# Idle products among the first scores, later empty rows, the last pair's first scores set between older value products, and four late transposes in one go, in an attention and mixture-of-experts kernel

## The chip, the cores and the metric

The kernel runs as one program on one core of a Trainium2 chip. The metric is the device time of that program in microseconds (us). Before the change three timed runs gave 710.47, 710.98 and 714.45 us, median 710.98 us. One further execution was profiled: it took 711.56 us, and the profile of it covers a span of 709.5 us from the first to the last instruction.

## The reference, cut to what matters

Attention over q, k, v of 4 batches, 8 heads, 768 tokens and 64 numbers per head. Each token gets six hash bits per head (the signs of a product with `proj`), and a query only sees keys of the same bucket. Every one of the 3072 tokens then goes to one of eight experts:

```python
mask = q_bucket[:, :, :, None] == k_bucket[:, :, None, :]
scores = np.where(mask, scale * np.matmul(q, k.transpose(0, 1, 3, 2)), -1e9)
attn = softmax(scores)                       # max, exp, sum, divide
x = np.matmul(attn, v)                       # tokens x 512 over all heads
expert_idx = np.argmax(x @ w_gate, axis=1)   # one expert per token
y[rows of e] = relu(x[rows of e] @ w1[e]) @ w2[e]
out = gate_w[:, None] * y
```

## The kernel before

**Pairs, units, halves.** The 32 heads are worked off in 16 pairs (`g` from 0 to 15, `NG` = 16). A pair has twelve units; a unit is 128 queries of one head against all 768 keys. Two heads' units make halves `u` = 2g and 2g+1 of the queries. For a unit, TensorE computes the scores into a PSUM tile "s" (`score`, lines 309 and 311: a sum of two products, since q and k are split into a high and a low part; the hash masks sit in sixteen extra rows of the split tile). VectorE takes the maximum (`peak`, L319) and two small factors (L324, L326; on some units GpSimd does them, L324 and L328), ScalarE takes the exponential (`expo`, L335). Half of the units are turned by TensorE transposes (`trans`, L349) and copied out (`trans_ev`, L375 on ScalarE or L373 on VectorE), the others by VectorE (`turn`, L389) and 16 DMAs from SBUF to SBUF (`exchange`, L400). The value products (`pv`, L411) collect six steps per half in a PSUM tile "t"; ScalarE copies the result (`pv_end`, L416), and `tok` (L430) brings it into token order. There are three "s" tiles and two "t" tiles.

**Masks.** The hash bits of a pair are computed one pair ahead (`lsh_mm`, L264), written to DRAM by SyncE (L278) and read back into the split tiles by two DMAs that GpSimd issues (`mask`, L282), behind its splitting work for the next pair (lines 192 to 233). The first score of a pair needs the mask of the pair's first head, and that is the later of the two reads. Pair 0 makes its bits in place (`lsh_first`, L239, `bits_first`, L250 on VectorE and L244 on ScalarE).

**What sets the order.** Each engine runs its own queue in order, and that order is written out by hand: a table of words per pair, read by `step`. `HEAD` is for pair 0, `PLAN` for pairs 1 to 14, `LAST` for pair 15. A word is a letter and a number: S score, R maximum, A factor, X exponential, T transpose, E its copy, B three steps of a value product, O its end, K and L the token product and its scaling, D and Y the VectorE turn and the exchange, Z and N routing; in `HEAD` also y (L239), b (bits), k j q l p (splitting) and f (the first score in two parts); in `LAST` also m, u, d (first expert: product, relu, its low part), n and t (a weight's high and low part, L941 and L949) and r, c (routing and scatter). A minus sign means the pair before, two mean the one before that. So "B11-" in the table of pair 14 is the second half of the value product of half 1 of pair 13.

**Empty rows.** Each expert has a region of rows in DRAM (`xs`, tile name "sorted_rows"). `fill(e)` (L150) writes 512 empty rows of expert e, one DMA of 1156 KB, issued on SyncE; `before`, called at every even score, says at which.

**First expert's rows.** Once all tokens are scattered, the rows of an expert are loaded (`rows`), transposed and split into a high and a low part (`xt`: L750 on TensorE, L755 on ScalarE, L756 on VectorE for the first expert's two groups of 256 rows; tile "xhe"), multiplied by w1 (`mm1`, L769) and by w2 (`mm2`, `yout`, L867), scaled (L878) and scattered to the output. Phases 0 and 1 are the two groups of the first expert. For phase 1 the kernel before transposes the first two of four blocks in the middle of the last w2 product of phase 0, and the other two behind it, all into "t" tiles:

```python
mm2(0, 1, lambda: xts(1, (0, 1)))
xts(1, (2, 3))
```

`warmth` (L106) issues products of a tile of ones with itself, 512 columns in bf16; ten of them run at the start.

Of the kernel before, what the change touches and what calls it, by code (L numbers as in the profile page):

```python
# [7 lines left out]
F32 = mybir.dt.float32  # L8
# [7 lines left out]
B, H, S, D = 4, 8, 768, 64  # L16
# [3 lines left out]
NG = B * NP  # L20
# [11 lines left out]
M0 = float(2 ** 34)  # L32
# [18 lines left out]
def tiles_of(n):  # L51

    return [(o, min(128, n - o)) for o in range(0, n, 128)]
# [3 lines left out]
def lsh_attention_moe(ctx, tc, qk2, v, proj, wg, w1, w1q, w2, out):  # L57
# [3 lines left out]
    ps = ctx.enter_context(tc.tile_pool(name="ps", bufs=1, space=bass.MemoryType.PSUM))  # L61
# [658 lines left out]
    def tokens(n):  # L720
        r, o, c = PH[n]
        IX[n] = moe.tile([128, 4], I32, name="ix", bufs=3)
        t = len(tiles_of(c))
        x = XI[n][:, :t, 1] if n > 1 else XG[n][:, :t, GC + 1]
        nc.vector.tensor_copy(IX[n][:, :t], x.bitcast(I32))

    def heads(x, d):

        return x[:, d * PW + E:d * PW + E + 2 * D]
# [9 lines left out]
    def xt(n, d):  # L739
        r, o, c = PH[n]  # L740
        if d == 0:
            XH[n] = (moe.tile([128, 2, 4, EARLY], F32R, name="xhe") if n < 2 else
                     P2["p"].tile([128, 2, 4, CAPS[1]], F32R, name="xh"))
        t = len(tiles_of(c))
        if n > 1:
            p = XT[n][:, d]
        else:
            p = ps.tile([128, 512], F32, name="t", bufs=2)
            for j in range(t):
                nc.tensor.transpose(p[:, j * 128:(j + 1) * 128], heads(XG[n][:, j], d), ident)  # L750
        if d == 0:
            GT[n] = moe.tile([128, 4], F32, name="gate", bufs=3)
            nc.vector.tensor_copy(GT[n][:, :t], XI[n][:, :t, 0] if n > 1 else XG[n][:, :t, GC])
            tokens(n)
        nc.scalar.activation(XH[n][:, 0, d, :c], p[:, :c], AF.Copy)  # L755
        nc.vector.tensor_tensor(XH[n][:, 1, d, :c], p[:, :c], XH[n][:, 0, d, :c], op=OP.subtract)  # L756

    LEN = {}

    def length(n):  # L760

        r = PH[n][0]
        LEN[n] = nc.values_load(C["ni"][0:1, r:r + 1], engines=[mybir.EngineType.PE], min_val=0, max_val=N)

    def products(n, p, c, terms):

        def part(z, ts, first):
            for k, (w, x) in enumerate(ts):
                nc.tensor.matmul(p[:, :z], w, x[:, :z], start=first and k == 0, stop=k == len(ts) - 1 and (n < 2 or not first))  # L769
# [5 lines left out]
        part(c, terms[:1], True)  # L775
        with tc.If(LEN[n] > z[2]) as more:
            with tc.If(LEN[n] > z[1]) as most:
                part(z[0], terms[1:], False)
            with most.Else():
                part(z[1], terms[1:], False)  # L780
        with more.Else():
            with tc.If(LEN[n] > z[3]) as some:
                part(z[2], terms[1:], False)
            with some.Else():
                part(z[3], terms[1:], False)

    XF = {}

    def xt_first(op, d):
        if op == "x":  # L790
            if not XF:
                XH[0] = moe.tile([128, 2, 4, EARLY], F32R, name="xhe")
            p = XF[d] = ps.tile([128, 2, 512], F32, name="s", bufs=3)
            for k in range(2):
                for j in range(2):
                    nc.tensor.transpose(p[:, k, j * 128:(j + 1) * 128], heads(XG[0][:, j], d + k), ident)
        elif op == "g":
            nc.scalar.activation(XH[0][:, 0, d:d + 2], XF[d][:, :, :EARLY], AF.Copy)
        else:
            nc.vector.tensor_tensor(XH[0][:, 1, d:d + 2], XF[d][:, :, :EARLY], XH[0][:, 0, d:d + 2], op=OP.subtract)  # L800

# [20 lines left out]
    M1 = {}  # L822
# [8 lines left out]
    def by_token(n):  # L831
        return PH[n][2] <= 384

    def mm2(n, m, mid=None):

        r, o, c = PH[n]
        if by_token(n):
            yout(n, m, mid)
            return
        if m == 0:  # L840
            YT[n] = (wk.tile([128, 4, EARLY], F32, name="qk") if n == 0 else
                     P2["p"].tile([128, 4, CAPS[1]], F32, name="yt"))
        h = HH[n]
        ms = slice(m * 128, (m + 1) * 128)
        p = ps.tile([128, 512], F32, name="s", bufs=3)
        if mid:
            mid()

        terms = [(CH[4 * r + 2 + f // 4][:, a, f % 4, ms], h[b][:, f]) for f in range(8) for a, b in ((0, 0), (0, 1), (1, 0))]
        products(n, p, c, terms)  # L850
        nc.scalar.activation(YT[n][:, m, :c], p[:, :c], AF.Copy)

    def yout(n, j, mid=None):
        r, o, c = PH[n]
        if j >= len(tiles_of(c)):
            return
        i, pw = tiles_of(c)[j]
        if n + 1 == len(PH) and j + 1 == len(tiles_of(c)):
            youts(n, j, i, pw)
            return  # L860
        p = ps.tile([128, 512], F32, name="s", bufs=3)
        if by_token(n):
            k = 0
            for f in range(8):
                w = CH[4 * r + 2 + f // 4]
                for a, b in ((0, 0), (1, 0), (0, 1)):
                    nc.tensor.matmul(p[:pw], HH[n][b][:, f, i:i + pw], w[:, a, f % 4],  # L867
                                     start=(k == 0), stop=(k == 23))
                    k += 1
                    if k == (12 if n else 20) and mid:  # L870
                        mid()
        else:

            yw = max(pw, min(128, CAPS[1] - i))
            for m in range(4):
                nc.tensor.transpose(p[:yw, m * 128:(m + 1) * 128], YT[n][:, m, i:i + yw], ident)  # L876
        y = (P2["p"] if n else moe).tile([128, DM], F32, name="y" if n else "ye", bufs=3 if n else 2)
        nc.vector.tensor_scalar(y[:pw], p[:pw], GT[n][:pw, j:j + 1], None, op0=OP.mult)  # L878
        nc.gpsimd.memset(C["spacer"], 0.0)
        st = nc.gpsimd.indirect_dma_start(out=out, out_offset=bass.IndirectOffsetOnAxis(ap=IX[n][:pw, j:j + 1], axis=0),  # L880
                                          in_=y[:pw], in_offset=None, bounds_check=N - 1, oob_is_err=False)
        for q in outs:
            tc.declare_no_dep(st.ins, q.ins, reason="rows of other tokens")
        outs.append(st)
# [47 lines left out]
    def weight_half(op, x):  # L932
# [21 lines left out]
    lows = []  # L954

    HEAD = """
        k01A k00V j00V j01P y01 q00A p00V y00 q01P l00V b03 p01P f0 b00 b02 l01P b01 k10A f1 k11A y11 j10P p10A R0
        q10A S1 j11P b12 y10 R1 l10P b13 S2 X0 b10 p11P s01 R2 X1 b11 S3 q11P S4 X2 G H w R3 T00 T01 E00a l11P S5 R4
        E01a T02 X3 s00 R5 E02a s02 T10 X4 S6 E10v X5 R6 T11 S7 s10 E11a T12 s13 R7 E12a T20 X6 S8 s03 E20v T21 X7
        S9 E21a T22 s11 R8 E22a D6 S10 s14 s15 s12 s05 s04 z0 z1 R9 X8 A9P D7 S11 R10 X9 A10P B00 D8 R11 A11P X10 B01 X11  # L960
    """.split()
# [1 line left out]
    PLAN = """  # L963
# [4 lines left out]
        B01  # L968
    """.split()

    LAST = """
        D9- D10- S0 D11- Y0- Y1- M0- O1-- O0- M1-- R0 K1-- L1-- K0- S1 X0 L0- R1 S2 S3 R2 X1 X2 S4 T00 T01 R3 E00a E01a R4 S5 X3 R5 T02 X4 X5 E02v
        T10 S6 E10a T11 T12 E11a R6 S7 T20 S8 R7 E12a T21 X6 S9 E20v X7 E21v B10- B11- O1- M1- M0 R8 T22 E22a x0 R9 X8 T30
        X9 g0 V0 E30a x2 h0 O0 T31 S10 g2 E31a T40 T32 h2 R10 E40a S11 T41 R11 E32a K0 E41v nA m0 L0 r0 X10 T42 X11 nA
        E42a T50 M1 tP E50a r0 m1 T51 nA r0 T52 E51a m2 E52a tP tV u0 u1 nP r0 tP u2 r0 r0 nA V1 d0 nP r0 O1 tP d1 K1-
        K1 m3 m4 d2 L1- L1 m5 r1 nP u3 r1 d3 r1 u4 d4 r1 nA r1 r1 m6 r1 u5 u6 tV c0 m7 u7 tV d5 d6 tP c1 d7
    """.split()

    def route_step(g, k):
# [21 lines left out]
    def before(c):  # L1001

        g, r = divmod(c, 6)
        if r == 3 and g + 2 < NG:
            load_x(2 * g + 4)
            load_x(2 * g + 5)
        if g + 1 < NG and r == (5 if g else 4):
            load_v(g + 1)
        for e in {(0, 1): (0,), (0, 2): (1,), (0, 3): (2,), (0, 4): (3,), (2, 4): (4,), (3, 4): (5,), (4, 4): (6,), (5, 4): (7,)}.get((g, r), ()):
            fill(e)  # L1010

    def behind(i):
# [97 lines left out]

    last = [route(B - 1, (0,)), route(B - 1, (1,))]
    for g in range(NG):
        for w in {0: HEAD, NG - 1: LAST}.get(g, PLAN):
            step(g, w)
            if (g, w) in PICK:
                next(pick, None)
                if w == PICK[-1][1]:
                    raw_load(0, 0)
                    raw_load(0, 1)
            if g == NG - 1 and w == "R9":  # L1120
                GT[0] = moe.tile([128, 4], F32, name="gate", bufs=3)
                nc.vector.tensor_copy(GT[0][:, :2], XG[0][:, :, GC])
                tokens(0)
# [6 lines left out]
    def xts(n, ds):  # L1130
        for d in ds:
            xt(n, d)

    mm2(0, 0)
    mm2(0, 1, lambda: xts(1, (0, 1)))
    xts(1, (2, 3))
    attn.close()
    p2 = ExitStack()
    P2["p"] = p2.enter_context(tc.tile_pool(name="p2", bufs=1))
# [18 lines left out]
    for n in range(1, len(PH)):  # L1158
        c0 = 4 * (PH[n][0] + 1)
# [31 lines left out]
    with tc.For_i(0, C["n"], 1) as i:  # L1191
# [16 lines left out]
        p = ps.tile([128, 512], F32, name="t", bufs=2)  # L1208
# [5 lines left out]
        for f in range(8):  # L1214
            p = ps.tile([128, 512], F32, name="t", bufs=2)
# [3 lines left out]
        p = ps.tile([128, 512], F32, name="s", bufs=3)  # L1219
# [32 lines left out]
```

## Time and profile before

| | before |
|---|---|
| timed runs, median | 710.98 us (710.47 to 714.45) |
| profiled execution | 711.56 us |
| its span | 709.5 us |
| busy: PE / DVE / ACT / POOL | 692.1 / 493.3 / 405.3 / 494.5 us |
| mean granted TensorE clock | 0.992 |
| pair 0 and the start | to about 34 us |
| pairs 1 to 14 | about 34 to 372 us, near 24 us each |
| pair 15 and the first expert's first group | about 372 to 434 us |
| experts, then the end | 434 to 709.5 us |

PE is TensorE, PEld its weight loads, DVE VectorE, ACT ScalarE, POOL GpSimd, SP SyncE. Times in the rows are us from the start of the span; a group of instructions that follow each other is one row with its start, its length, and in brackets the idle time of the engine before it and what ended that. The clock is the share of full speed that TensorE was granted: 1.00 is 2.4 GHz and 0.50 is 1.2 GHz.

### The profile page before, as it was taken

Reading aid. Unit: us, or ns where it says so; the run is one execution under the profiler, and the core shown is the slowest. Engines: PE = TensorE matmul, PEld = TensorE weight load, DVE = VectorE, ACT = ScalarE, POOL = GpSimd, SP = SyncE. Lnnn points to the kernel's source line nnn. Section 1 sums busy time; section 2 is a strip of 40 time slices with the busy share of each in tenths; the row PEclk is TensorE's granted clock in tenths of the full one; section 3 lists DMA queues with packets and bytes.
Section 4 is the critical chain, followed back from the end, with each engine's and each line's share of the span. In section 5 each row is a group of like instructions: output and inputs, shape, how many; then the busy total and the mean of one; then the engine's idle time right before and its main releaser. Section 6 shows DMA issues by size and latency. Waiting matters only on the chain.

```text
span 709.5 us, 13598 instructions
## 1 busy us (share of the span) xinstructions
PE 692.1 (98%) x4539; PEld 558.2 (79%) x4539; DVE 493.3 (70%) x925; ACT 405.3 (57%) x813; POOL 494.5 (70%) x763
## 2 busy tenths in 40 slices
PE   8899999999999999999998999999999999999996
PEld 4677668767876786677666778899999999989895
DVE  7988898899888998898988662424766825332321
ACT  5786678667766786687666723544444444444310
POOL 8875686688777787886884564675666676768522
PEclk8999999999999999999999999999999999999998
DMA  8886889887966687777668238683847474747201
GB/s 320 285 245 173 252 249 244 257 245 223 284 183 206 197 221 235 220 228 222 187 182 265 89 131 214 198 232 114 196 137 185 139 196 139 204 154 207 90 12 39
DMA packets 67774, 138.32 MB, mean 195 GB/s; under 512 B 12883, under 2 KB 29523, under 8 KB 67680
## 3 DMA queue, kind: packets, MB, share of 16 engines
q1 hardware_dynamic: 60848, 120.67, 60.2%
q0 software_dynamic: 6688, 16.35, 6.7%
q8 instruction: 61, 1.00, 0.6%
q14 instruction: 33, 0.27, 0.1%
q10 hardware_dynamic: 144, 0.03, 0.0%
HBM read 75.79 MB, written 26.33 MB: 144 GB/s over the span
## 4 chain that ended last, share of the span: by engine, by line
PE 83%; issue 5%; POOL 4%; ACT 3%; DVE 3%; DMA 1%; another core or an unknown queue 0%; POOLq 0%; ACTq 0%; DVEq 0%
PE s L769 28%; PE t L411 18%; PE s L309 9%; PE s L867 8%; PE s L311 7%; PE t L349 7%; PE t L430 3%; ACT e L335 2%; PE t L264 2%; DVE m L319 1%; PE s L876 1%; DMA w<-masks 1%; ACT pt L375 1%; POOL w L694 1%; PE t L106 1%
## 5 line engine op out<-in xcount | busy, mean ns | idle before, releaser
L335 ACT ACTIVATE e<-s,m 128x768 f32<-128x768 f32 x192 | 189.6, 991 | 59.4 <-POOL m L328 41.0
L319 DVE TENSOR_REDUCE m<-s 128x1 f32<-128x768 f32 x192 | 180.1, 950 | 31.9 <-PE s L311 26.3
L694 POOL TENSOR_TENSOR w<-raw,w 128x512 fp32r<-128x512 f32 x112 | 145.0, 1319 | 32.9 <-ACT w L693 31.8
L411 PE MATMUL t<-pt,vt 128*64 128x384 f32 x768 | 130.9, 490 | 1.5 <-ACT e L335 1.5
L769 PE MATMUL s<-xh,w 128*128 128x432 f32 (+11 forms) x672 | 121.8, 338 | 0.0
L769 PEld LDWEIGHTS s<-xh,w 128*128 128x128 f32 x672 | 114.6, 188 | 3.0 <-issue 0.6
L411 PEld LDWEIGHTS t<-pt,vt 128*64 128x64 f32 x768 | 52.5, 137 | 65.8 <-issue 62.1
L829 DVE SCALAR_TENSOR_TENSOR hh<-s,hh 128x256 fp32r<-128x256 f32 (+7 forms) x64 | 35.5, 555 | 95.0 <-ACT hh L827 93.6
L349 PE MATMUL t<-ident,e 128*128 128x128 f32 x612 | 87.7, 276 | 2.5 <-ACT e L335 1.1
L389 DVE STREAM_TRANSPOSE w<-e 128x768 f32<-128x768 f32 x90 | 82.8, 954 | 1.6 <-ACT e L335 1.0
L827 ACT ACTIVATE hh<-s 128x256 fp32r<-128x256 f32 (+7 forms) x64 | 31.3, 489 | 91.2 <-PE s L769 91.2
L349 PEld LDWEIGHTS t<-ident,e 128*128 128x128 f32 x612 | 70.1, 141 | 13.5 <-ACT pt L375 3.4
L769 PE MATMUL s<-hh,w 128*128 128x432 f32 (+5 forms) x384 | 72.3, 349 | 0.0
L769 PEld LDWEIGHTS s<-hh,w 128*128 128x128 f32 x384 | 69.9, 188 | 1.3
L693 ACT ACTIVATE w<-raw 128x512 fp32r<-128x512 f32 x112 | 66.7, 623 | 7.2 <-DMA raw<-in_w1q_dram 5.2
L324 POOL TENSOR_SCALAR m<-m 128x1 f32<-128x1 f32 x115 | 26.4, 229 | 61.9 <-DVE m L319 59.5
L880 POOL DMA_INDIRECT out_dram<-y,ix x26 | 26.9, 1033 | 59.1 <-DVE y L878 22.8
L309 PE MATMUL s<-w 80*128 80x384 f32 x192 | 57.0, 378 | 2.7 <-ACT e L335 1.6
L309 PE MATMUL s<-qk 80*128 80x384 f32 x192 | 57.7, 383 | 1.8 <-ACT e L335 1.7
L867 PE MATMUL s<-w,hh 128*128 128x512 f32 (+1 forms) x240 | 56.4, 394 | 0.0
L375 ACT ACTIVATE pt<-t 128x512 f32<-128x512 f32 (+1 forms) x96 | 53.6, 586 | 4.4 <-PE t L349 2.5
L867 PEld LDWEIGHTS s<-w,hh 128*128 128x128 f32 (+1 forms) x240 | 44.6, 187 | 10.5
(222 smaller groups left out, 1069.6 us busy)
## 6 DMA issues: line engine op xcount, KB each, us to landing
pt<-w SPq DMA_DIRECT2D x240, 144.0 KB
raw<-in_w_dram SPq DMA_DIRECT2D x36, 512.0 KB
raw<-in_w1q_dram SPq DMA_DIRECT2D x28, 512.0 KB
w<-in_qk_dram SPq DMA_DIRECT2D x14, 768.0 KB
xd<-in_qk_dram SPq DMA_DIRECT2D x14, 768.0 KB
sorted_rows<-xr SPq DMA_DIRECT2D x8, 1156.0 KB
vt<-in_v_dram SPq DMA_DIRECT2D x16, 384.0 KB
xg<-sorted_rows SPq DMA_DIRECT2D x16, 256.0 KB
```

The costliest lines, as they stand in the source:

```text
L309: nc.tensor.matmul(p[:, a, :HALF], k[0:80, 2, c], k[0:80, 3, n], start=i >= 4, stop=i < 4)
L311: nc.tensor.matmul(p[:, a, :HALF], k[:, 0, c], k[:, 1, n], start=i < 4, stop=i >= 4)
L319: nc.vector.tensor_reduce(m[:, 0:1], p[:, :, :HALF], axis=AX.XY, op=OP.max, negate=True)
L335: nc.scalar.activation(e, p[:, :, :HALF], AF.Exp, bias=m[:, 2:3], scale=m[:, 1:2], accum_out=SM[g, hf][:, t, s:s + 1])
L349: nc.tensor.transpose(p[:, x * 128:(x + 1) * 128], e[w][:, kt // 3, (kt % 3) * 128:(kt % 3) * 128 + 128], ident)
L375: nc.scalar.activation(o, x, AF.Copy)
L389: nc.vector.transpose(d.rearrange("p b k q -> p k b q"), PP.pop(i).rearrange("p a c -> p (a c)"))
L411: nc.tensor.matmul(p[s * 64:(s + 1) * 64, :HALF], VT[g][:, kt, s, :], x, start=(kt == 0), stop=(kt == NT - 1))
L693: nc.scalar.activation(w[:, 0, a], r, AF.Copy)
L694: nc.gpsimd.tensor_tensor(w[:, 1, a], r, w[:, 0, a], op=OP.subtract)
L769: nc.tensor.matmul(p[:, :z], w, x[:, :z], start=first and k == 0, stop=k == len(ts) - 1 and (n < 2 or not first))
L867: nc.tensor.matmul(p[:pw], HH[n][b][:, f, i:i + pw], w[:, a, f % 4], start=(k == 0), stop=(k == 23))
```

## The change

Five edits.

1. `HEAD`: eleven idle products (`warmth` on score tiles, words i02, i02, i13, i11, i11, i21, i21) stand among the hash products and scores of units 0 to 2. A score that follows starts its sum anew, so they leave nothing behind.
2. `before`: the empty rows of expert 2 are written one step earlier, behind those of expert 1; those of expert 3 move from pair 0 to pair 1.
3. `TURN` is a new table for pair 14, and `LAST` is rewritten at its start: the second half of the value product of pair 13 (B11) and of pair 14 (B01) go from pair 14's end to between the first scores of pair 15. The last unit's factor in pair 14 goes from GpSimd to VectorE.
4. The end of `LAST`: d5 (the low part of the sixth relu, L829) stands ahead of the weights' low parts; one of these moves from GpSimd to VectorE (tP becomes tV).
5. `xt` and its call: all four transposes of phase 1 stand in the middle of the w2 product, the last two into one "s" tile.

```diff
-            p = ps.tile([128, 512], F32, name="t", bufs=2)
+            if d == 2:
+                XF[n] = ps.tile([128, 2, 512], F32, name="s", bufs=3)
+            p = ps.tile([128, 512], F32, name="t", bufs=2) if d < 2 else XF[n][:, d - 2]
...
-        k01A k00V j00V j01P y01 q00A p00V y00 q01P l00V b03 p01P f0 b00 b02 l01P b01 k10A f1 k11A y11 j10P p10A R0
+        k01A k00V j00V j01P y01 q00A p00V i02 y00 q01P l00V b03 p01P i02 f0 b00 b02 l01P b01 k10A i13 f1 k11A i11 y11 j10P p10A R0
...
+    TURN = " ".join(PLAN).replace(" B11-", "").replace("R11", "R11 A11V").replace("A11P ", "").rsplit(" ", 1)[0].split()
...
-        D9- D10- S0 D11- Y0- Y1- M0- O1-- O0- M1-- R0 K1-- L1-- K0- S1 X0 L0- R1 S2 S3 R2 X1 X2 S4 T00 T01 R3 E00a E01a R4 S5 X3 R5 T02 X4 X5 E02v
+        D9- D10- S0 B11-- D11- Y0- Y1- O1-- R0 S1 S2 X0 R1 K1-- M1-- L1-- B01- O0- X1 R2 S3 K0- R3 M0- L0- X2 T00 T01 E00a S4 E01a R4 S5 X3 R5 T02 X4 X5 E02v
...
-        K1 m3 m4 d2 L1- L1 m5 r1 nP u3 r1 d3 r1 u4 d4 r1 nA r1 r1 m6 r1 u5 u6 tV c0 m7 u7 tV d5 d6 tP c1 d7
+        K1 m3 m4 d2 L1- L1 m5 r1 nP u3 r1 d3 r1 u4 d4 r1 nA r1 r1 m6 r1 u5 d5 u6 tV c0 m7 u7 tV tV d6 c1 d7
...
-        for e in {(0, 1): (0,), (0, 2): (1,), (0, 3): (2,), (0, 4): (3,), (2, 4): (4,), (3, 4): (5,), (4, 4): (6,), (5, 4): (7,)}.get((g, r), ()):
+        for e in {(0, 1): (0,), (0, 2): (1, 2), (1, 4): (3,), (2, 4): (4,), (3, 4): (5,), (4, 4): (6,), (5, 4): (7,)}.get((g, r), ()):
...
-        for w in {0: HEAD, NG - 1: LAST}.get(g, PLAN):
+        for w in {0: HEAD, NG - 2: TURN, NG - 1: LAST}.get(g, PLAN):
...
-    mm2(0, 1, lambda: xts(1, (0, 1)))
-    xts(1, (2, 3))
+    mm2(0, 1, lambda: xts(1, range(4)))
```

Three places show what moves. TensorE at the start of pair 0, behind the ten products of ones; L239 are the hash products of pair 0, L311 and L309 the two parts of its first score. The four hash products stood together before:

```order
L239 MATMUL t<-xd,pj 32x384 x4
L311 MATMUL s<-qk 128x384 x2
L309 MATMUL s<-qk 128x384 x2
L239 MATMUL t<-xd,pj 32x384 x2
L311 MATMUL s<-qk 128x384 x2
```

Now:

```order
L239 MATMUL t<-xd,pj 32x384 x2
L106 LDWEIGHTS ones
L106 MATMUL s<-ones 128x512
...
L239 MATMUL t<-xd,pj 32x384 x2
...
L311 MATMUL s<-qk 128x384 x2
...
L309 MATMUL s<-qk 128x384 x2
```

Each line of dots leaves out idle products. Two idle products part the first two hash products from the next two; two more stand ahead of the first score's L311 part, three between its parts, and four around the other hash products.

TensorE where pair 14 ends and pair 15 begins, before: behind the last score of pair 14 (qk) come 18 value products in a row (B00, B11 and B01, six each), and then the scores of pair 15 (w_4693 is its first head, w_4586 its second):

```order
L309 MATMUL s<-qk 128x384 x2
L311 MATMUL s<-qk 128x384 x2
L411 MATMUL t<-pt,vt 64x384 x18
L309 MATMUL s<-w_4693 128x384 x2
L311 MATMUL s<-w_4693 128x384 x2
L430 MATMUL t<-wgt,ot 128x144 x6
L309 MATMUL s<-w_4586 128x384 x2
L311 MATMUL s<-w_4586 128x384 x2
```

And now (w_4708 the first head, w_4601 the second):

```order
L411 MATMUL t<-pt,vt 64x384 x6
L309 MATMUL s<-w_4708 128x384 x2
L311 MATMUL s<-w_4708 128x384 x2
L411 MATMUL t<-pt,vt 64x384 x6
L309 MATMUL s<-w_4601 128x384 x2
L311 MATMUL s<-w_4601 128x384 x2
L309 MATMUL s<-w_4708 128x384 x2
L311 MATMUL s<-w_4708 128x384 x2
L430 MATMUL t<-wgt,ot 128x144 x3
L411 MATMUL t<-pt,vt 64x384 x6
L309 MATMUL s<-w_4601 128x384 x2
L311 MATMUL s<-w_4601 128x384 x2
```

The first score of pair 15 follows B00 alone; B11 stands behind it, B01 behind the third score and a token product.

VectorE at the end of pair 15, before: the weights' low parts (L949) ahead of the low parts of three relus (L829; d5, d6 and d7):

```order
L490 TENSOR_REDUCE slot<-pb 128x3
L492 TENSOR_REDUCE rf<-ex 128x3
L494 RECIPROCAL xr<-rf 128x3
L949 TENSOR_TENSOR w_5329<-raw,w_5329 128x512 x2
L829 SCALAR_TENSOR_TENSOR qk<-s,qk 128x256 x3
```

And now:

```order
L490 TENSOR_REDUCE slot<-pb 128x3
L492 TENSOR_REDUCE rf<-ex 128x3
L494 RECIPROCAL xr<-rf 128x3
L829 SCALAR_TENSOR_TENSOR qk<-s,qk 128x256
L949 TENSOR_TENSOR w_5344<-raw,w_5344 128x512 x3
L829 SCALAR_TENSOR_TENSOR qk<-s,qk 128x256 x2
```

d5 goes ahead of the weights, and there are three of these.

## Rows read from the trace of the kernel before

**Rows 1.** The page's first part: busy us, share of the span, instructions.
```profile
PE 692.1 (98%) x4539; PEld 558.2 (79%) x4539; DVE 493.3 (70%) x925; ACT 405.3 (57%) x813; POOL 494.5 (70%) x763
```
**Rows 2.** Windows: stretch, length, busy PE, PEld, DVE, ACT, POOL, clock, DMA share, GB/s.
```profile
5.40:9.20 3.80, 3.03 (x18) 1.09 (x17) 3.63 (x5) 2.92 (x7) 3.64 (x5) 1.00 0.91 341
9.20:16.00 6.80, 6.80 (x22) 4.98 (x20) 4.64 (x12) 4.28 (x8) 6.43 (x9) 0.50 1.05 384
...
384.30:417.00 32.70, 32.70 (x240) 24.89 (x240) 20.63 (x57) 17.93 (x38) 17.56 (x22) 1.00 0.41 137
```
**Rows 3.** The chain of waits around the end of pair 0: start, us, what.
```profile
27.27 6.55 DMA w<-masks
...
33.96 0.58 PE s L309 x2
```
**Rows 4.** Timeline of PE at the start: start, us, instruction, count.
```profile
1.07 4.45 PE L106 MATMUL t<-ones 128*128 128x512 bf16 x10 [1.07 <-DVE warm L98]
5.45 1.04 PE L239 MATMUL t<-xd,pj 64*32 64x384 f32 x8
...
8.40 0.83 PE L239 MATMUL t<-xd,pj 64*32 64x384 f32 x4
```
**Rows 5.** Timeline of DVE: unit 5's maximum in pair 0, unit 0's in pair 1.
```profile
19.55 0.96 DVE L319 TENSOR_REDUCE m<-s 128x1 f32<-128x768 f32 x1 [0.88 <-ACT pt L375]
...
34.94 0.96 DVE L319 TENSOR_REDUCE m<-s 128x1 f32<-128x768 f32 x1 [0.29 <-PE s L311]
```
**Rows 6.** Timeline of POOL: unit 9's factor in pair 0, mask read for pair 15.
```profile
28.65 0.26 POOL L324 TENSOR_SCALAR m<-m 128x1 f32<-128x1 f32 x1
...
367.29 0.60 POOL L282 DMA_DIRECT2D w<-masks  x1
```
**Rows 7.** Timeline of ACT: units 9 and 11 of pair 0, unit 1 of pair 15.
```profile
29.22 0.99 ACT L335 ACTIVATE e<-s,m 128x768 f32<-128x768 f32 x1 [1.04 <-POOL m L328]
...
32.28 0.99 ACT L335 ACTIVATE e<-s,m 128x768 f32<-128x768 f32 x1 [0.64 <-POOL m L328]
...
376.61 0.99 ACT L335 ACTIVATE e<-s,m 128x768 f32<-128x768 f32 x1 [1.27 <-DVE m L326]
```
**Rows 8.** DMA queues from 27.3 to 31 us: packets, MB, share of 16 engines.
```profile
q1 hardware_dynamic: 543, 1.28, 103.2%
```
**Rows 9.** DMA queues from 367.3 to 369.4 us.
```profile
q0 software_dynamic: 80, 0.10, 20.0%
```
**Rows 10.** Timeline of PE from the end of pair 14 into pair 15.
```profile
365.80 6.03 PE L411 MATMUL t<-pt,vt 128*64 128x384 f32 x36
371.75 0.62 PE L309 MATMUL s<-w 80*128 80x384 f32 x2
...
372.56 1.63 PE L430 MATMUL t<-wgt,ot 128*128 128x144 f32 x12
...
377.74 0.62 PE L309 MATMUL s<-w 80*128 80x384 f32 x2 [1.38 <-ACT e L335]
...
383.74 0.66 PE L349 MATMUL t<-ident,e 128*128 128x128 f32 x4 [0.63 <-ACT pt L375]
```
**Rows 11.** Timeline of PE where the first expert's first group ends.
```profile
421.24 10.54 PE L867 MATMUL s<-w,qk 128*128 128x512 f32 x44 [0.64 <-DVE qk L829]
431.61 0.60 PE L750 MATMUL t<-ident,xd 128*128 128x128 f32 x4
431.96 1.18 PE L867 MATMUL s<-w,qk 128*128 128x512 f32 x4
...
434.20 6.00 PE L769 MATMUL s<-xhe,w 128*128 128x256 f32 x48 [0.45 <-ACT xhe L755]
```
**Rows 12.** Timeline of DVE there: weights' low parts, the second group's gates.
```profile
419.55 1.29 DVE L949 TENSOR_TENSOR w<-raw,w 128x512 fp32r<-128x512 f32 x2
...
430.51 0.17 DVE L753 COPY gate<-xd 128x2 f32<-128x2 f32 x1 [2.63 <-DMA xd<-sorted_rows]
```
**Rows 13.** Timeline of ACT there: the first two high parts.
```profile
432.08 0.66 ACT L755 ACTIVATE xhe<-t 128x256 fp32r<-128x256 f32 x2 [11.07 <-PE t L750]
```

More of the change, by code (lines that the diff above doesn't have):

```diff
@@ L756, in xt @@
         nc.vector.tensor_tensor(XH[n][:, 1, d, :c], p[:, :c], XH[n][:, 0, d, :c], op=OP.subtract)
-    LEN = {}
+    LEN, XF = {}, {}
     def length(n):
@@ L785, in products @@
                 part(z[3], terms[1:], False)
-    XF = {}
     def xt_first(op, d):
@@ L956, in lsh_attention_moe @@
     HEAD = """
-        k01A k00V j00V j01P y01 q00A p00V y00 q01P l00V b03 p01P f0 b00 b02 l01P b01 k10A f1 k11A y11 j10P p10A R0
-        q10A S1 j11P b12 y10 R1 l10P b13 S2 X0 b10 p11P s01 R2 X1 b11 S3 q11P S4 X2 G H w R3 T00 T01 E00a l11P S5 R4
+        k01A k00V j00V j01P y01 q00A p00V i02 y00 q01P l00V b03 p01P i02 f0 b00 b02 l01P b01 k10A i13 f1 k11A i11 y11 j10P p10A R0
+        q10A i11 S1 j11P b12 i21 y10 R1 l10P b13 i21 S2 X0 b10 p11P s01 R2 X1 b11 S3 q11P S4 X2 G H w R3 T00 T01 E00a l11P S5 R4
         E01a T02 X3 s00 R5 E02a s02 T10 X4 S6 E10v X5 R6 T11 S7 s10 E11a T12 s13 R7 E12a T20 X6 S8 s03 E20v T21 X7
```

## The prediction, on record before the run

> **What bounds the kernel now.** I read the page's busy shares first: TensorE is busy for 692.1 us, 98% of the span, no other engine for more than 70% [rows 1]. So time comes out of the kernel only where TensorE waits or is slow. The windows by stage show where that is. From 384.3 to 417 us it is busy for 32.70 of 32.70 us, so whatever is won or lost ahead of that is carried to the end unchanged [rows 2]. From 9.2 to 16 us it is just as busy, but at a granted clock of 0.50, the lower of its two levels; in the 3.8 us before, at 1.00, it stood idle for 0.77 [rows 2]. The chain of waits gives the reason for the end of pair 0: it runs through GpSimd into a read of masks, issued at 27.27 us and 6.55 us long, and the first score of pair 1 starts behind it at 33.96 [rows 3]. The timeline of TensorE shows the other places: waits of 1.38 and 0.63 us in pair 15 [rows 10], of 0.64 and 0.45 us where the first expert's first group ends [rows 11].
>
> **The head: idle products and empty rows.** The slow 6.8 us hold 3.4 us of work at full clock. If the idle products keep the clock up, up to 3.4 come back. Against that stand eleven idle products. At full clock I take 0.24 us each, from 44 products of the same 512 columns in 10.54 us [rows 11]: 2.6 us, of which 0.77 fall into the idle time [rows 2]. At the lower level it is 0.445 each, as for the first ten, 4.45 us [rows 4]. They also part the hash products: eight records, four hash products run as one group, took 1.04 us, four records alone 0.83 [rows 4], so apart they take 0.6 more. TensorE gains 3.4 − 1.8 − 0.6 = 1.0 us.
>
> The Trainium skill, in "TensorE: Matmul & The Clock Gate", Part 3 (packing small matmuls), says that products at different tile positions of the array run concurrently; the trace agrees, with 1.04 us for eight records against 0.83 for four. By that rule alone, with no clock won back, this edit would only cost.
>
> What arrives further on? VectorE had 0.88 us of idle time before the maximum of unit 5, which waited for a score queued behind late transposes [rows 5]; TensorE 1.0 us earlier removes about 0.9 of it, and from there VectorE is nearly back to back to the maximum of unit 0 of pair 1 at 34.94. GpSimd sets a cap: it makes the factor of unit 9 only at 28.65, behind both reads of masks [rows 6], so the exponential of unit 9 stays at 29.22; with 0.99 each, unit 11 could end at 32.19 at best instead of 33.27 [rows 7], 1.1 us earlier. And the masks must be there 0.9 us earlier. During the read the hardware queue filled the DMA engines (103.2%) [rows 8]; a read with nothing beside it, for pair 15, was issued at 367.29 [rows 6], and all its 80 packets were through by 369.4, about 2.1 us [rows 9]. The change takes the 1156 KB for expert 3 off the queue and sends expert 2's earlier. Between 2.1 and 6.55 us I take 4, which is early enough; the price of the extra write behind pair 1 is nothing, since there the queue has no reader waiting that I found. The head term is −0.9 us; bounds −1.1 (the cap) and, with the clock falling all the same, +3.7 (below).
>
> On that read the skill's "DMA: Bandwidth & Descriptors", section on queues, rings and completion order, says that an engine takes turns between queue rows packet by packet. By it a read on another row should hardly feel the megabytes queued on SyncE's; then moving them wins nothing and the head term is 0. The trace has 6.55 us beside 2.1, which speaks for a cost of the load, but two reads were issued at once in the slow case.
>
> **Pair 14 into pair 15.** B00 takes a third of 36 records in 6.0 us, 2.0 us [rows 10], so the first score of pair 15 now comes up at 367.8 instead of 371.75. But the mask it needs is issued at 367.29 by a GpSimd that is busy until then [rows 6] and lands at about 369.4 [rows 9]. A wait of 1.6 us appears that was hidden under B11 and B01 before. Then: score 0.8 (370.2), B11 2.0 (372.2), two scores 1.5 (373.7; the first took 0.8 to the next start), a token product 0.8, half of twelve records in 1.63 [rows 10] (374.5), B01 2.0 (376.5). On ScalarE the copy of B01's result stands ahead of the exponential of unit 1, so that one starts at about 377.0; before it started at 376.61 [rows 7]. What it waited for, VectorE, now has time, but the copy of the value product is what is late next. Half of that 0.4 us I let pass on (the rest is a guess at ScalarE's slack between there and unit 5), so the wait of 0.63 us at 383.74 for ScalarE [rows 10] stays, 0.2 us later. The 1.38 us wait turns into the 1.6 us one. The factor of unit 11 on VectorE takes two short instructions out of GpSimd's queue and lets the last exponential and the exchange start earlier; nothing waits for them. Term: +0.2 us; bounds −1.15 (no wait for the mask: everything 1.6 earlier, until VectorE binds) and +0.8 (mask 0.6 later).
>
> **The first expert.** d5 ahead of the weights frees a score tile before TensorE wants it: the wait of 0.64 us goes [rows 11]. Behind it d6 and d7 come one weight part later, 0.65 us (half of 1.29 [rows 12]); their products are the last of eight in a sum of 5 us, so these wait for nothing. But VectorE ranks the experts behind d7, and SyncE loads the second group's rows behind that; they arrived at 430.5 [rows 12], and TensorE wants them at 431.6 − 0.6 = 431.0. Arriving at 431.15, they cost 0.15. If the load hung on the scatter instead, they cost nothing.
>
> The four transposes: before, the last two came behind the product, which ran to 433.1, and the next phase waited for ScalarE until 434.20 [rows 11]. Now all eight records stand ahead of the last four products: 431.61 + 0.45 + 0.45 + 1.0 = 433.5 (four records took 0.35 to the next start and 0.60 to their own end; four products of 0.24), while ScalarE makes the four high parts from 432.08 on at 0.33 each, to 433.4 [rows 13]. The next phase can start at 433.5: −0.7 us. It is the "s" tile that makes it possible; the phase's second score tile waits only for work that is done by then. Term: −0.6 − 0.7 + 0.1 = −1.2 us; bounds −1.4 and −0.4 (the rows late by the full 0.65, and part of the second gain with them).
>
> **Sum.** −0.9 + 0.2 − 1.2 = −1.9 us. Against the profiled execution's 711.56 us (span 709.5) that is 709.66; that execution was 0.58 above the median of the runs, so the forecast for the median is 710.98 − 1.9 = 709.1 us, 0.27% below.
>
> **Rivals.**
> *The clock falls as before, slower than before.* Something in the first 9 us let it fall at 9.2, and idle products between two fast stretches need not cure it. It decides from the point where it falls under the idle products: with five of them before and six after, they cost 5 × 0.24 + 6 × 0.445 = 3.9, less 0.77, plus 0.6 for the parted hash products, and nothing comes back: +3.7, all of it on the way to the maximum of unit 5. With the other two terms: +2.7, 713.7 us. For it: the idle time before the fall was only 0.77 us of 3.8 [rows 2], so idleness may not be the whole cause. Against it: the ten products of the same kind ran just before, and the clock stood at 1.00 behind them until that idle stretch.
> *The head gives nothing.* The read of masks still lands at 33.8, by packets taking turns or because two reads at once are slow anyway; unit 0 of pair 1 starts where it did. Then 0.2 − 1.2 = −1.0: 710.0 us. Against it rows 8 beside rows 9.
> *The last pair's first score does not wait.* If GpSimd comes to the mask read earlier, the change does what its order suggests: −1.15 in place of +0.2, sum −3.25, 707.7 us. For it only that pair 14's GpSimd queue might run ahead; against it [rows 6], where the read is the last of a busy stretch.
>
> **How the numbers follow.** Forecast 709.1: 0.52, its own range 708.2 to 710.2 by the terms' smaller errors. Head gives nothing: 0.20. The mask in time: 0.13. The clock falls: 0.12. Something else: 0.03. A measurement here can tell about 0.5%, 3.6 us, from no change: faster than 707.4 needs every bound at once (−1.1 − 1.15 − 1.4 = −3.65), with some room for what I have not seen: 0.13. Slower than 714.5 needs the falling clock and a bad term beside it: 0.05. The rest, 0.82, lies within. The range runs from 706.9, a little below the case without the mask's wait, to 712.0, which leaves out the falling clock.
>
> **What the profile after would show.** Right: a granted clock near 1.00 between 9 and 16 us, and the first score of pair 1 near 33.0; a wait of TensorE for a DMA of masks ahead of the first score of pair 15, some 1.6 us; no wait for VectorE's low part at the first w2 product; no wait for ScalarE behind the transposes. Wrong: a clock of 0.50 in the first 16 us; the first score of pair 1 not earlier; no mask wait in pair 15, or its first exponential after 377.5; the second group's rows late.

## The result: 0.55% slower

The changed kernel took 715.14 us (median of 13 runs, 713.78 to 718.28), the kernel before 711.49 beside it (13 runs, 709.72 to 714.45). The ratio is 1.0055, 95% interval 1.0042 to 1.0067: 3.65 us slower by the medians, 3.9 by the ratio, where 709.1 was forecast and 706.9 to 712.0 was the range. Compared a second time it came to 1.0080 (1.0056 to 1.0104). The profiled execution was the longest of its 13 (718.28 us, span 716.5), so its stretches are read one by one below and not summed against the median.

**The head.** The windows of the changed kernel that answer to [rows 2], one around the first score of pair 1 and one in pair 15; the columns are the same.

```profile
5.40:9.20 3.80, 3.80 (x20) 1.55 (x20) 3.33 (x5) 2.86 (x6) 3.64 (x5) 1.00 0.99 361
9.20:16.00 6.80, 6.55 (x59) 3.78 (x55) 5.82 (x12) 4.92 (x10) 6.43 (x9) 1.00 1.05 383
27.00:40.00 13.00, 10.56 (x77) 6.53 (x78) 9.26 (x15) 5.76 (x14) 7.40 (x15) 0.87 0.70 183
372.00:380.00 8.00, 7.63 (x36) 4.61 (x38) 4.25 (x11) 1.46 (x3) 7.53 (x10) 0.79 0.41 141
```

The clock of 0.50 between 9 and 16 us is gone and TensorE gets to the end of pair 0 earlier: its products there start at 28.09 instead of 29.13 us. But the first score of pair 1 [rows 3] is no earlier. In the timeline of TensorE (start, us, instruction, in brackets the idle time before it and its releaser) it starts at 34.43 behind a wait of 2.26 us for the mask, and the clock falls in the stretch around it (0.87).

```profile
28.09 4.09 PE L411 MATMUL t<-pt,vt 128*64 128x384 f32 x24
...
34.43 0.71 PE L309 MATMUL s<-w 80*128 80x384 f32 x2 [2.26 <-DMA w<-masks]
```

**Pair 14 into pair 15.** From the kernel before, the last score of pair 14 and the first transpose of the expert's rows; between them lie [rows 10], and one more short wait.

```profile
364.89 0.62 PE L309 MATMUL s<-qk 80*128 80x384 f32 x2
...
381.30 0.44 PE L349 MATMUL t<-ident,e 128*128 128x128 f32 x2 [0.35 <-ACT e L335]
...
391.82 0.60 PE L796 MATMUL s<-ident,xd 128*128 128x128 f32 x4
```

The same stretch of the changed kernel:

```profile
367.13 0.61 PE L309 MATMUL s<-qk 80*128 80x384 f32 x2
...
368.03 2.16 PE L411 MATMUL t<-pt,vt 128*64 128x384 f32 x12
372.37 0.72 PE L309 MATMUL s<-w 80*128 80x384 f32 x2 [2.19 <-DMA w<-masks]
...
373.66 3.34 PE L411 MATMUL t<-pt,vt 128*64 128x384 f32 x12
...
384.44 0.66 PE L349 MATMUL t<-ident,e 128*128 128x128 f32 x4 [0.95 <-ACT pt L375]
...
389.18 0.66 PE L349 MATMUL t<-ident,e 128*128 128x128 f32 x4 [1.10 <-DVE pt L373]
390.27 0.65 PE L349 MATMUL t<-ident,e 128*128 128x128 f32 x4 [0.43 <-ACT pt L375]
...
398.35 0.60 PE L796 MATMUL s<-ident,xd 128*128 128x128 f32 x4
```

From score to transpose, call it the turn: 26.93 us before, 31.22 after, +4.3. The new wait for the mask is there, the waits further on come to 2.48 us instead of 2.36, and behind the mask's wait a value product of 12 records takes 3.34 us instead of 2.16: the window from 372 to 380 us above has a clock of 0.79.

**The first expert**, to be laid beside [rows 11]:

```profile
426.96 10.43 PE L867 MATMUL s<-w,qk 128*128 128x512 f32 x44
437.23 0.27 PE L752 MATMUL t<-ident,xd 128*128 128x128 f32 x1
437.91 0.55 PE L752 MATMUL t<-ident,xd 128*128 128x128 f32 x3 [0.41 <-DMA xd<-sorted_rows]
438.30 0.38 PE L752 MATMUL s<-ident,xd 128*128 128x128 f32 x2
439.89 0.44 PE L752 MATMUL s<-ident,xd 128*128 128x128 f32 x2 [1.22 <-DVE xhe L758]
...
441.11 3.14 PE L771 MATMUL s<-xhe,w 128*128 128x256 f32 x25
```

The wait of 0.64 for VectorE is gone, but a new one of 1.22 stands inside the four transposes. From the first transpose of rows to the next phase's first product, call it the tail: 42.38 us before (391.82 to 434.20), 42.76 after.

### The profile page after: what moved, and what is told of

Read it like the earlier page. It is cut to its first block, busy times and chain, and to the rows that moved or that the text cites. A ratio compares the mean times of both kernels' runs of the same rounds, so it can differ in the third digit from the quotient of the medians.

```text
span 716.5 us, 13622 instructions
## 1 busy us (share of the span) xinstructions
PE 694.8 (97%) x4550; PEld 558.2 (78%) x4550; DVE 493.7 (69%) x928; ACT 405.2 (57%) x813; POOL 493.5 (69%) x760
## 5 line engine op out<-in xcount | busy, mean ns | idle before, releaser
L411 PE MATMUL t<-pt,vt 128*64 128x384 f32 x768 | 132.5, 494 | 1.7 <-ACT e L335 1.7
L829 DVE SCALAR_TENSOR_TENSOR hh<-s,hh 128x256 fp32r<-128x256 f32 (+7 forms) x64 | 35.5, 555 | 97.2 <-ACT hh L827 95.1
L309 PE MATMUL s<-w 80*128 80x384 f32 x192 | 57.4, 380 | 4.8 <-DMA w<-masks 4.4
L309 PE MATMUL s<-qk 80*128 80x384 f32 x192 | 56.7, 377 | 1.7 <-ACT e L335 1.0
```

Source lines behind the costliest of these rows:

```text
L309: nc.tensor.matmul(p[:, a, :HALF], k[0:80, 2, c], k[0:80, 3, n], start=i >= 4, stop=i < 4)
L411: nc.tensor.matmul(p[s * 64:(s + 1) * 64, :HALF], VT[g][:, kt, s, :], x, start=(kt == 0), stop=(kt == NT - 1))
L829: nc.vector.scalar_tensor_tensor(h1[:, f, :c], p[:, :c], 0.0, h0[:, f, :c], op0=OP.max, op1=OP.subtract)
```

## The experiments

Theory A: the loss is the turn (the mask's wait and the clock behind it). B: it is the head. C: it is the late transposes. Each part of the change was first put alone on the kernel before. Each ratio is to the kernel before, timed beside it.

**The parts alone.** `idle`: only the eleven idle products (in the first two lines of `HEAD`).

> The kernel before with the eleven idle products alone; the fills of empty rows, pair 14 into 15 and the first expert stay as they were. Theory A (the loss sits between pair 14 and 15): the clock in the first 16 us is cured, but the first score of pair 1 still waits for its mask, so at most 0.5 us moves: ratio 0.999 to 1.001. Theory B (the loss sits in the head: TensorE now stands still for 2.3 us in front of that mask, and its clock falls behind it): 1 to 3 us slower, ratio 1.002 to 1.004. Theory C (the loss sits in the late transposes): as A.

`fills`: only the line that sets when empty rows are written.

> The kernel before with the moved writes of empty rows alone. Theory A: the read of the first pair's masks lands where it did, near 33.8 us, since the SyncE queue's load in the window is not what it waits for: ratio 0.9995 to 1.0005. Theory B: the same or up to 0.5 us slower (the earlier write of expert 2 pushes the loads behind it). My step on record would have had the read land 2.5 us earlier, near 31.3, with the first score of pair 1 held by the exponential of unit 11 instead: up to 0.5 us faster, ratio 0.9993.

`turn`: only the new table and the start of the last one.

```
+    TURN = " ".join(PLAN).replace(" B11-", "")...
-        D9- D10- S0 D11- Y0- Y1- M0- O1-- ...
+        D9- D10- S0 B11-- D11- Y0- Y1- O1-- ...
```

> The kernel before with only the new order around pair 14 into pair 15 (value products of pairs 13 and 14 moved behind the first scores of pair 15; factor of unit 11 on VectorE). Theory A: the whole loss, 2.5 to 4.5 us slower, ratio 1.0035 to 1.0063: TensorE waits about 2.2 us for the mask in front of pair 15's first score, its clock falls behind that, and the expert starts 3 to 4 us later. Theory B: 0 to 0.8 us slower, ratio up to 1.0011. Theory C: as B.

`tail`: only the end of the last table, and the four transposes with their shared score tile.

> The kernel before with only the first expert's changes (d5 ahead of the last weight halves; four transposes in one go inside the last product's sum). Theory A: from the start of the expert to the second phase's first product about 0.4 us later than before, ratio 1.000 to 1.001. Theory C (rows of the second group late, and the shared score tile makes the fourth transpose wait for VectorE): 1.2 us or more slower, ratio 1.0015 to 1.003. My step on record would have it 1.2 us faster, 0.9983.

Measured: `idle` 1.0011 (0.9994 to 1.0028), `fills` 1.0009 (0.9990 to 1.0029), `tail` 1.0011 (0.9995 to 1.0027), `turn` 1.0055 (1.0031 to 1.0080). In `fills` the step on record for the writes did come out: the two reads of masks, issued at 27.6 and 28.3 us, land within 3.8 us, and the first score of pair 1 starts at 33.58 without a wait, behind TensorE's own queue.

```profile
33.58 0.62 PE L309 MATMUL s<-w 80*128 80x384 f32 x2
```

The turn alone is as slow as the whole change: A stands, B and C fall as the main cause. The reverse, `noturn`, is everything but the turn:

> The changed kernel without the new order around pair 14 into pair 15: idle products, fills and first expert as changed. Theory A: the three small parts together cost next to nothing: ratio 0.9995 to 1.002. Theories B and C together: 1.003 or more. If the parts' medians add (0.11 + 0.09 + 0.11%): 1.003.

Measured 1.0003 (0.9985 to 1.0021): nothing clear of noise is left. The timeline of `turn`, where the clock stays up, prices the wait and the order by themselves:

```profile
364.40 0.61 PE L309 MATMUL s<-qk 80*128 80x384 f32 x2
...
365.29 2.16 PE L411 MATMUL t<-pt,vt 128*64 128x384 f32 x12
369.60 0.58 PE L309 MATMUL s<-w 80*128 80x384 f32 x2 [2.15 <-DMA w<-masks]
...
380.06 0.66 PE L349 MATMUL t<-ident,e 128*128 128x128 f32 x4 [0.95 <-ACT pt L375]
...
384.80 0.66 PE L349 MATMUL t<-ident,e 128*128 128x128 f32 x4 [1.09 <-DVE pt L373]
385.89 0.66 PE L349 MATMUL t<-ident,e 128*128 128x128 f32 x4 [0.43 <-ACT pt L375]
...
393.98 0.60 PE L796 MATMUL s<-ident,xd 128*128 128x128 f32 x4
```

The turn is 29.58 us, +2.65. Before, it holds waits of 1.38, 0.35 and 0.63, in sum 2.36; here the later waits alone are 2.47, and the mask's 2.15 come on top. The remaining 0.4 or so is a difference and not a row; that it lies in the groups of products that are now cut into smaller ones is my guess.

**The clock's share.** `turn_fill`: `turn` with eight idle products in the wait.

```
-        D9- D10- S0 B11-- D11- ...
+        D9- D10- I8 S0 B11-- D11- ...
```

> The new order around pair 14 into pair 15 alone, with eight idle products of 512 columns ahead of pair 15's first score, written into its tile and overwritten by it: TensorE does no useful work in the wait for the mask, but does not stand still. Theory A: the wait's 2.15 us stay, the falling clock behind it goes: all runs near the better ones of the part alone (712.4), ratio 1.003 to 1.004 and a narrower spread. If the clock has no part in it: 1.0055 as before.

Measured 1.0038 (1.0024 to 1.0053), 712.71 to 715.73 us where `turn` ranged from 712.37 to 718.25. Its turn is 29.57 us (366.30 to 395.87):

```profile
369.28 1.90 PE L106 MATMUL s<-ones 128*128 128x512 bf16 x8
371.49 0.58 PE L309 MATMUL s<-w 80*128 80x384 f32 x2 [0.31 <-DMA w<-masks]
```

The same on the whole change, side by side with it:

> The changed kernel once more, to be compared with the next in the same rounds: 1.0055 within 0.0015, about 714 to 715.5 us.

> The changed kernel with eight idle products ahead of pair 15's first score. If the clock that falls behind the wait is a part of the loss (theory: 2.66 us of waits and order, the rest clock): 1 to 2 us faster than the changed kernel, 1.003 to 1.004 of before, and fewer executions above 715. If the waits alone make the loss: no difference.

Measured 1.0080 (1.0056 to 1.0104) and 1.0057 (1.0044 to 1.0070). The turns of their profiles are 31.23 us and 29.60. The window from 385 to 390 us, first of the one without idle products, then of the one with them:

```profile
385.00:390.00 5.00, 4.57 (x22) 4.20 (x21) 2.67 (x7) 3.14 (x8) 0.00 (x0) 0.66 0.87 271
```

```profile
385.00:390.00 5.00, 3.48 (x24) 2.88 (x23) 3.56 (x9) 4.36 (x8) 0.00 (x0) 1.00 0.92 245
```

The clock is 0.66 in the first, where the turn is long, and 1.00 in the second. So the turn has two lengths, 29.6 without a falling clock and 31.2 with one, 1.6 us apart; the two profiles with idle products in the wait show the shorter, as does that of `turn` without any. The fall need not come in the wait itself: here it comes some 16 us later, behind the waits of 1.10 and 0.43. The profiles of two kernels below have this late fall too, with 0.66 in the same window: `turn_zx`, and `turn_half`, whose wait for the mask is only 0.20. So the idle products stand at one of the two places where the clock fell; that they keep it up at the other is not shown. In times the two pairs of ratios point the same way (0.17 and 0.23%), but their intervals overlap. The mean granted clock of each execution says more on how often it falls: of the 13 of the changed kernel, three at 0.998 or 0.999 took 713.78 to 714.39 us, seven at 0.996 714.00 to 717.34, and three at 0.993 717.67 to 718.28. The first three are 2.6 us above the median before, about what `turn` loses with the clock up; where in an execution the clock was low, such a mean does not tell.

**The mask's read.** `turn_z`: `turn` with the read ahead of two low parts and a factor in GpSimd's queue.

```
-    TURN = " ".join(PLAN).replace(" B11-", "")...
+    TURN = " ".join(PLAN).replace(" B11-", "").replace(" z0", "").replace("C04", "C04 z0")...
```

> The new order around pair 14 into pair 15, as in the run of that part alone, but with GpSimd's read of pair 15's first mask put ahead of two low parts and a factor, so that it is issued about 2.4 us earlier. Theory A (the loss is the 2.15 us wait for that mask, and the clock that falls behind it in part of the runs): the wait goes, and of the 0.55% some 0.1% is left: ratio 1.000 to 1.0015. Rival D (the order itself costs: ScalarE copies a value product's result ahead of the second exponential, and later waits grow by what the mask's wait gives back): first score 2 us earlier but waits of 4 us or more behind it, ratio 1.003 to 1.005.

Measured 1.0027 (1.0012 to 1.0042), half of the loss. GpSimd's timeline and TensorE's:

```profile
365.63 0.54 POOL L282 DMA_DIRECT2D w<-masks  x1 [0.29 <-POOL w L214]
```

```profile
369.15 0.58 PE L309 MATMUL s<-w 80*128 80x384 f32 x2 [0.79 <-DMA w<-masks]
```

The wait shrinks from 2.15 to 0.79 and the turn from 29.58 to 28.21, by just as much. A put the rest at 0.1%; it is 0.27, so A was not all: the later waits (0.95, 1.10, 0.43) stand unchanged. The read, begun 2.1 us earlier, takes 3.5 us to the score instead of 2.8. Two repairs of the later waits, one after the other: `turn_zx` puts the exponential of unit 1 ahead of the copy of the value product (`B01- X1 O0-` for `B01- O0- X1`), and `turn_zxs` also the fifth score ahead of the transposes (`X2 S4 T00 T01 E00a` for `X2 T00 T01 E00a S4`).

> As the kernel with the earlier mask read, and also the exponential of pair 15's second score ahead of the copy of pair 14's first value result on ScalarE. Theory A: the 0.95 us wait for ScalarE ahead of the second late transpose goes or halves; 0 to 1.5 us faster than the kernel before, ratio 0.998 to 1.000. Rival D: this, and not the mask's read, gives the larger step: 2 us or more below the kernel with the earlier read alone.

> The new order around pair 14 into pair 15 with three repairs: mask read earlier, second exponential ahead of the copy, and the fifth score of pair 15 back in front of the first late transposes, so that VectorE's maximum of it does not wait. Theory A with the later waits named: the 0.8 us VectorE idles for that score and a good part of the 1.10 us wait for VectorE's copy go; level with the kernel before or up to 1 us faster: ratio 0.9985 to 1.0005. If the waits behind are set by something else: 1.0016 as without the third repair.

Measured 1.0016 (1.0000 to 1.0032) and 1.0009 (0.9993 to 1.0024). The waits behind the mask are 0.69, 1.10 and 0.43 with the first, 0.61, 0.30 and 0.58 with both; by these waits the second repair is the larger, while the ratios do not part them. The turn of `turn_zx` is 29.63 instead of 28.21, with the late fall of the clock in it. With both, the mask's wait was 1.38 in its profile, 4.10 us from issue to score, and the turn 28.14: an earlier read alone does not make the mask early.

**The score later instead.** `turn_half`: pair 13's value product back in front of the first score, the read where it was (`B11-- S0` for `S0 B11--`); `half_xs`: that with the two repairs.

> The new order around pair 14 into pair 15 with the value product of pair 13 back in front of pair 15's first score: that score comes up 2.1 us later, when its mask has just landed, and only one value product is moved behind it. Theory A: no wait, no falling clock: ratio 0.9995 to 1.0015. Rival D (the order on ScalarE and VectorE behind costs): 1.002 to 1.004.

> The new order with pair 13's value product back in front of pair 15's first score (mask read where it was), the second exponential ahead of the copy and the fifth score ahead of the late transposes. Level with the kernel before or up to 1 us faster, ratio 0.9985 to 1.0005; if only the mask's wait mattered, 1.001 as without these two.

Measured 1.0010 (0.9994 to 1.0026) and 0.9995 (0.9979 to 1.0012). The turn of `turn_half` is 28.90, with the late fall of the clock in it. `half_xs`, TensorE:

```profile
366.60 0.61 PE L309 MATMUL s<-qk 80*128 80x384 f32 x2
...
371.81 0.59 PE L309 MATMUL s<-w 80*128 80x384 f32 x2 [0.23 <-DMA w<-masks]
...
380.40 0.66 PE L349 MATMUL t<-ident,e 128*128 128x128 f32 x4 [0.62 <-DVE xr L440]
...
382.72 0.44 PE L349 MATMUL t<-ident,e 128*128 128x128 f32 x2 [0.30 <-ACT e L335]
...
385.15 0.66 PE L349 MATMUL t<-ident,e 128*128 128x128 f32 x4 [0.58 <-ACT pt L375]
...
393.24 0.60 PE L796 MATMUL s<-ident,xd 128*128 128x128 f32 x4
```

The turn is 26.64, 0.29 shorter than before: the idea of the change, with the mask's wait and the two orders taken out, is worth that.

**The late transposes.** `late4`: the kernel before with the four transposes in one go, but those of parts 2 and 3 both ahead of the copies out of their shared score tile (the evictions). Cut to the call:

```
-    mm2(0, 1, lambda: xts(1, (0, 1)))
-    xts(1, (2, 3))
+    mm2(0, 1, lambda: (xts(1, (0, 1)), xt(1, 2, 0), xt(1, 3, 0), xt(1, 2, 1), xt(1, 3, 1)))
```

(0 makes the transposes alone, 1 the evictions.)

> The kernel before with the four late transposes in one go inside the last product's sum, but with the transposes of parts 2 and 3 both ahead of the evictions of part 2, so that part 3's write into the shared score tile does not come behind VectorE's read of part 2. Theory (the shared tile made the wait of 1.22 us): the wait goes, the second phase's first product comes 12.3 us behind the first product of the sum that is last but one, instead of 12.96 before and 13.5 with the tile's wait: 0.6 us faster, ratio 0.999 to 1.0. Rival (the wait is VectorE's own work queued there): the 1.22 us stay in another place, ratio 1.001.

Measured 0.9992 (0.9978 to 1.0006); TensorE:

```profile
421.42 10.53 PE L869 MATMUL s<-w,qk 128*128 128x512 f32 x44
431.79 0.60 PE L752 MATMUL t<-ident,xd 128*128 128x128 f32 x4
432.23 0.60 PE L752 MATMUL s<-ident,xd 128*128 128x128 f32 x4
...
433.59 6.65 PE L773 MATMUL s<-xhe,w 128*128 128x256 f32 x54
```

The 1.22 us wait is gone; from L869 to the next phase 12.17 us against 12.96 before. The tail is 40.90 us here, 42.11 in `tail`, 42.12 to 42.13 in `noturn`, `after_again` and `after_fill`, and 41.69 to 41.77 in the nine other kernels that have the old one; only the profile of the kernel before had 42.38, with the 0.64 us wait in it.

**The pieces together.** `best1` is `half_xs` with `late4`; `best2` has the head's two edits as well.

> The kernel before with two repaired parts: the new order around pair 14 into pair 15 with pair 13's value product ahead of the first score, the second exponential ahead of the copy and the fifth score ahead of the late transposes; and the late transposes in one go with both evictions behind. The profiles of the two parts had -0.29 and -0.79 us: 1.1 us faster, ratio 0.9985, within 0.997 to 1.000. If they do not add: 0.9995.

> The same with the idle products and moved fills of the head as well. If the head's part gains what its profile has from the first score of pair 1 on (nothing to 0.4 us lost, clock kept in part): as the one before, 0.998 to 0.9995. If the idle products gain in the middle of executions: 0.9975.

Measured 0.9988 (0.9976 to 1.0000; 710.38 us beside 711.38) and 0.9998 (0.9981 to 1.0015). Both have a turn of 26.6 to 26.7 and a tail of 40.9. `best1` is at the edge of being faster than the kernel before; no gain from the head shows on top of it.

## Why the prediction was wrong

**The turn is the step that failed**: +0.2 forecast, with an upper bound of 0.8; 2.65 in the profile with the clock up, 4.3 with a fall. With 0.4 from the tail and nothing from the head that makes 3.1 or 4.7 us; the measured 3.65 lies between. Three sentences of it were off.

"A wait of 1.6 us appears": 2.15 to 2.19. [Rows 9] told when the mask's packets were through, and I took that for the landing. In `turn` the read is issued at 366.79. That row, and two windows of the DMA queues there, 367.9 to 368.9 and 368.9 to 369.7 us:

```profile
366.79 0.60 POOL L282 DMA_DIRECT2D w<-masks  x1
```

```profile
q0 software_dynamic: 80, 0.10, 39.3%
```

```profile
DMA packets 0, 0.00 MB, mean 0 GB/s; under 512 B 0, under 2 KB 0, under 8 KB 0
```

All 80 packets are through by 368.9, none moves for 0.7 us, and only then, at 369.60, does the score start. From issue to score it was 2.80 to 2.82 us in the changed kernel, `turn`, `turn_fill`, `turn_half` and `half_xs`, whatever the score's place (2.90 in `best1`): the term should have been 2.8, not 2.1. The Trainium skill, in "DMA: Bandwidth & Descriptors", section on the anatomy of one DMA, says that the semaphore cannot fire before the last byte is confirmed in the target memory; the trace agrees as far as the 0.7 us without packets go.

"The 1.38 us wait turns into the 1.6 us one", and 0.63 "stays": the order behind the score has waits of its own. ScalarE, in `turn`:

```profile
377.08 0.49 ACT L416 ACTIVATE ot<-t 128x384 f32<-128x384 f32 x1 [2.95 <-PE t L411]
377.47 0.99 ACT L335 ACTIVATE e<-s,m 128x768 f32<-128x768 f32 x1
```

I had named this copy as what is late next, but priced it at 0.2 by the start of one exponential. Counted from pair 14's last score, that exponential starts at 13.07 us against 11.72 before, and VectorE then waits for the fifth score, which was moved behind the transposes:

```profile
381.46 0.96 DVE L319 TENSOR_REDUCE m<-s 128x1 f32<-128x768 f32 x1 [1.08 <-PE s L311]
```

With both put back, and pair 13's value product ahead of the first score (`half_xs`), waits of 0.23, 0.62, 0.30 and 0.58 are left of 4.62.

And the clock: I had a fall only in the head as a rival, none behind a wait that the change itself makes. It costs 1.6 us where it comes.

**The head**: −0.9 forecast, no gain measured; a gain of this size is not excluded by `noturn`, whose interval reaches down to 0.9985. Both steps came out in part. The writes: in the window of [rows 8], 27.3 to 31 us, in which none of the read's packets moved before, the changed kernel moves most of its 160.

```profile
q0 software_dynamic: 144, 0.18, 33.1%
```

Over all profiles the read's packets begin at 28.7 to 29.2 us in the six kernels with the moved writes, `fills` among them, and at 31.7 to 32.6 in the twelve without (in the kernel before 4.4 us after the issue); the last one starts at 31.1 to 34.0 instead of 33.8 to 35.9. So the read did stand behind the writes, and the rival by which it lands at 33.8 whatever the writes do is out, though in the profile of the changed kernel the last few packets come only at 34.0.

The clock: with idle products pair 1's first score starts at 34.43, 32.51, 32.62 and 33.20, but twice at 36.59; without them at 33.58 to 35.03 in the eight profiles whose clock is low for some 7 us, and at 35.19 to 35.60 in four where it is low for longer. Two things work against the gain. The mask's wait is 2.26 us in one execution of the changed kernel and 0.40 in another; in the latter the score is 1.45 us earlier than before, so the cap of 1.1 that I took from ScalarE did not bind it. And in `idle` and `noturn`, the two with 36.59, the products run at half speed until 13.3 us. The windows there read a clock of 1.00 only because a stretch without any clock record counts as 1.00: the records of these two begin at 13.8 us, those of the other four with idle products at 3.8 to 5.8. `idle`, TensorE and the window:

```profile
5.45 1.49 PE L239 MATMUL t<-xd,pj 64*32 64x384 f32 x4
6.87 1.03 PE L106 MATMUL s<-ones 128*128 128x512 bf16 x2
7.83 1.49 PE L239 MATMUL t<-xd,pj 64*32 64x384 f32 x4
```

```profile
5.00:9.00 4.00, 4.00 (x12) 0.50 (x10) 2.01 (x3) 2.42 (x5) 3.52 (x5) 1.00 0.99 376
```

Four records take 1.49 here; eight took 1.04 in [rows 4]. Why full speed comes near 5 us in most profiles and at 13.8 in these two is open; without idle products two of twelve, `turn_fill` and `turn_half`, have their first clock record only at 17.3. The executions of `idle` and `noturn` came near the rival of the slow clock, too: their score is 2.6 us later than before, of its 3.7, and they were 2.1 and 3.1 us above the medians of their kernels. In the times, "the head gives nothing" came nearer than my forecast, but not for the reason it gave. What held back the read's last packets cannot be said: the DMA engines are nearly idle from 31 to 34 us in the profile of the changed kernel, with only 15 packets of GpSimd's queue left.

**The first expert**: −1.2 forecast, +0.4 measured (42.12 against 41.70). The sum "431.61 + 0.45 + 0.45 + 1.0" let the four transposes run one behind the other. But part 3's write the tile of which VectorE still reads part 2, and wait 1.22 us for it; `late4`, where the evictions come behind all transposes, gets the 0.7 forecast and a little more, 0.8. A tile of its own for each part was not tried. The 0.64 for d5 was a row of one execution: 426.96, the product behind it, starts without a wait, but so does this one of `turn`, whose code there is that of before:

```profile
422.71 10.53 PE L867 MATMUL s<-w,qk 128*128 128x512 f32 x44
```

Its worth is what is left, 0.1 us: from the first transpose of rows to this product it is 28.59 us in `tail` and 28.72 to 28.74 in `idle`, `fills` and `turn`. The second group's rows were late by 0.41 in one profile and not in `tail`.

**The rivals.** The turn's worst end, 0.8, came from moving the mask alone; the bound should have held every later wait that the new order can open, and a fall of the clock behind each; with 4 us there, slower by over 0.5% would have had more than 0.05. That the mask comes in time, the rival with the other sign, is excluded by the 2.15 us.

## What to carry on

When work is moved ahead of a transfer, take the time to the waiting instruction's start from a case where one waits, not the time of the last packet, and read the order behind it engine by engine: the wait that you remove at one place is often paid by the next three. Put reads of one score tile behind all writes to it. And before a stall of one profile becomes a term of a sum, look for it in a second execution.

## What the hardware showed that I had not expected

The same code takes the same time to 0.03 us where nothing stalls: the turn was 26.90 to 26.93 us in six kernels, and the old tail 41.69 to 41.71 in eight. From the hash products of one pair (L264) to those of the next, ten of the thirteen steps between pairs 1 and 14 agree to 0.07 us over all 18 profiles. Only those from pairs 1, 6 and 10 vary, from 23.6 to 27.5, 23.8 to 25.3 and 23.8 to 25.6 us, with and without the change: the spread between the profiles there comes from these three. One wait for a mask moved from 2.26 to 0.40 between two executions of one kernel. And TensorE came to full speed at 3.8 to 6.8 us in fourteen profiles, at 13.8 in two and at 17.3 in two, while the windows before that read 1.00: where a half-speed row stands beside a clock of 1.00, look for the first clock record.
